# Regrouping a decode-attention kernel: K and V in four 4 MB units, four heads to a score bank, the FFN moved before the last values

## The chip, the cores and the metric

One NeuronCore of one Trainium2 chip; the other cores are idle. The metric is device time in microseconds (us) of one execution. A profile's span is not the time measured for the same execution, so spans are compared with spans here, and times with times.

Engines: PE multiplies matrices, DVE is the vector engine, ACT the scalar engine, POOL sets constants, SP asks for the loads. DMA is 16 engines that all loads share.

An execution is called *slow* when it is over 1.5% longer than the fastest of its kernel.

## The reference, cut to what matters

```python
xn = layernorm(x)                                   # x: (2, 1, 448)
q  = (xn @ wq)                                      # 16 heads of 256
k, v = k_cache[:, :, -2048:], v_cache[:, :, -2048:] # 2 batches, 8 kv heads, 2048 x 256 each
s  = softmax(q . k / 16) . v                        # two q heads share a kv head
s  = s.reshape(2, 1, 4096) @ wo                     # wo: (4096, 448)
g  = silu(relu(xn @ w1) @ w2)                       # w1: (448, 1792)
out = x + s * g
```

All inputs are bf16. K and V are 16.8 MB each, wq and wo 3.7 MB each, w1 and w2 1.6 MB each: 44.1 MB in all, each byte used once. The line of `g` is called the FFN below. The work is small, the bytes are not.

## The kernel before

Every operation is put into a list for its engine, with the operations that it waits for; an engine executes its list in order. A head pair `k` is one kv head for both batches; its K and V come as 1 MB transfers, 8 KB to a partition:

```python
def kv_src(c, cache):
    hkv, b = divmod(c, 2)
    return cache[b, hkv, SK - W:SK, :].rearrange("(p t) d -> p (t d)", t=NT)   # NT = 16
```

K is transposed on PE (`do_T`, four fp32-viewed 128x128 transposes into a bank, a piece of the memory that PE writes to, then one eviction, a copy out of it, by DVE or ACT in turn), multiplied with q (`do_S`, into bank `sbk`), put through a softmax (maximum over all keys by a transpose of the row maxima on PE, bias, exp, sum), and p is transposed and multiplied with V (`do_PV`). Here is the table of steps, which threads the parts of one pair between the transposes of the next ones:

```python
for i in range(NCH * NPAIR):
    at_step(i, 0, lambda i=i: do_T(i))
...
for k in range(NPAIR):
    e = NCH * k                                  # NCH = 8 transpose groups a pair
    at_step(e + 8, 2, lambda k=k: do_S(k, 0))
    at_step(e + 11, 2, lambda k=k: do_S(k, 1))
    at_step(e + 11, 4, lambda k=k: ch_max(k))
    at_step(e + 12, 4, lambda k=k: ch_rmT(k))
    at_step(e + 13, 4, lambda k=k: ch_bias(k))
    at_step(e + 13, 4, lambda k=k: ch_exp(k))
    at_step(e + 16, 4, lambda k=k: ch_Pt(k))
    at_step(e + 17, 4, lambda k=k: ch_sum(k))
    # ... do_PV from step e + 18 on, two of its groups at a time
```

After the last pair come `do_H(0)`, `do_H(1)`, `do_hT`, `do_F` (the FFN: 14 matmuls of 448 columns, seven small ones, 56 of 112), then wo (128 matmuls). The loads are asked for in the order K, V, ..., w1, w2, wo.

Of the kernel before, what the change touches and what calls it, by code (L numbers as in the profile page):

```python
# [5 lines left out]
BF = mybir.dt.bfloat16  # L6
# [70 lines left out]
def bass_recurrent_scan__sliding_block_cached__dense_activation_relu__decode_kernel(  # L77
# [21 lines left out]
    NT = W // 128  # L99
    NPAIR = HKV  # L100
    NCH = 8
    SLOTS = 7
    NKB = 6
    NVB = 8
    NKT = 12
    NP = 3
    HC = HD // 2
    FC = DFF // 2
    WO_PARTS = [10, 10, 8, 2, 2]
    NCOL = D // 4  # L110

    es = contextlib.ExitStack()
    with es:
# [17 lines left out]
        qmask = named("qmask", [128, 4], F32)  # L131
        fold = named("fold", [128, 32], BF)
        gsum = named("gsum", [128, 128], F32)
# [8 lines left out]
        qz = named("qz", [128, 16 * NPAIR], BF)  # L142
# [7 lines left out]
        rm = [named(f"rm{i}", [128, 1], F32) for i in range(2)]  # L150
        mrow = [named(f"mrow{i}", [128, 128], F32) for i in range(2)]
        bias = [named(f"bias{i}", [128, 1], F32) for i in range(2)]
        e_sb = [named(f"e_sb{i}", [128, 512], BF) for i in range(2)]
        ssum = [named(f"ssum{i}", [128, 1], F32) for i in range(2)]
        rs = named("rs", [128, NPAIR], F32)
        pt = [named(f"pt{i}", [128, 64], BF) for i in range(NP)]
        o_sb = [named(f"o_sb{i}", [128, 512], BF) for i in range(2)]
        at_exp = named("at_exp", [128, 256], BF)
        at2 = named("at2", [128, 64], BF)
        wqo = named("wqo", [128, 32 * D], BF)  # L160
        assert SLOTS * HC <= 32 * D
        w1_sb = named("w1_sb", [128, SLOTS * FC], BF)
        w2_sb = named("w2_sb", [128, 14 * D], BF)
        kbuf = [named(f"kbuf{i}", [128, NT * DH], BF) for i in range(NKB)]
        vbuf = [named(f"vbuf{i}", [128, NT * DH], BF) for i in range(NVB)]
        kt = [named(f"kt{i}", [128, 1024], BF) for i in range(NKT)]
# [11 lines left out]
        def kv_src(c, cache):  # L178
            hkv, b = divmod(c, 2)
            return cache[b, hkv, SK - W:SK, :].rearrange("(p t) d -> p (t d)", t=NT)  # L180

# [4 lines left out]
        d_k, d_v = {}, {}  # L186
        last_T, last_PV = {}, {}

        wq_src = A_wq.rearrange("r (hf c) -> (r hf) c", hf=2).rearrange("(p s) c -> p (s c)", s=SLOTS)
        w1_src = B_w1.rearrange("r (hf c) -> (r hf) c", hf=2).rearrange("(p s) c -> p (s c)", s=SLOTS)  # L190
        w2_src = B_w2.rearrange("(hf p j) n -> p hf (j n)", hf=2, j=7)
        wo_src = A_wo.rearrange("(p j) n -> p (j n)", j=32)

        def load_k(c):
            d_k[c] = pr.dma(SP, kbuf[c % NKB][:, :], kv_src(c, A_k_cache), [last_T.get(c - NKB)])

        def load_v(c):
            d_v[c] = pr.dma(SP, vbuf[c % NVB][:, :], kv_src(c, A_v_cache), [last_PV.get(c - NVB)])

        load_k(0)  # L200
        load_k(1)
        d_wq = pr.dma(SP, wqo[:, 0:SLOTS * HC], wq_src)
        load_k(2)
        load_k(3)
# [10 lines left out]
        p_mr = [pr.op(POOL, lambda e, t=t: e.memset(t[0:1, :], 0.0)) for t in mrow][-1]  # L215
        p_qz = pr.op(POOL, lambda e: e.memset(qz[:, :], 0.0), [p_one])

        a_z = [pr.op(ACTE, lambda e, t=t: e.memzero(t[:, :])) for t in (obk[0], sbk, obk[1], fbk)]  # L218
# [20 lines left out]
        def fold_op(e):  # L239
            with nc.allow_low_precision("zeros and ones"):  # L240
                return e.tensor_reduce(out=fold[:, :], in_=view(ident, 0, [[1, 32], [32, 4]]), axis=AX.X, op=ALU.add)
        v_fold = pr.op(DVE, fold_op)
        v_gs = pr.op(DVE, lambda e: e.tensor_copy(
            view(gsum, 0, [[32, 4], [1, 32]]), view(fold, 0, [[0, 4], [1, 32]])), [v_fold])
# [5 lines left out]
        for s in range(SLOTS):  # L250
# [4 lines left out]
            in1=view(par8, 0, [[1, SLOTS], [1, 2], [0, 2]]), op=ALU.mult), [m_xr, v_par8])  # L255

        evac, last_S, freed = {}, {}, set()
        st = {}

        def do_T(i):  # L260
            k, s = divmod(i, NCH)
            c = 2 * k + s // 4
            bank, src = tb[i % 3], kbuf[c % NKB]
            src_f, bank_f = src[:, :].bitcast(F32), bank[:, :].bitcast(F32)
            deps = [d_k[c], p_idf, evac.get(i - 3)]
            for n in range(4):
                lo = (4 * (s % 4) + n) * (DH // 2)
                o = pr.op(PE, lambda e, n=n, lo=lo: e.matmul(  # L268
                    bank_f[:, n * 128:(n + 1) * 128], lhsT=src_f[:, lo:lo + 128], rhs=ident_f[:, :],
                    start=True, stop=True, is_transpose=True), deps)  # L270
                deps = []
            last_T[c] = o
            if s % 4 == 3:
                freed.add((load_k, c))
            dst = kt[i % NKT]
            deps = [o, last_S.get(i - NKT)]
            if i % 2 == 0:
                evac[i] = pr.op(DVE, lambda e: e.tensor_copy(dst[:, :], bank[:, :]), deps)  # L278
            else:
                evac[i] = pr.op(ACTE, lambda e: e.activation(dst[:, :], bank[:, :], ACT.Copy), deps)  # L280

        def do_S(k, b):
            bank = sbk
            deps = [st["q"], a_z[1]] + ([st["exp", k - 1]] if b == 0 and k else [])
            for dhi in range(2):
                lhsT = qz[:, 16 * k + 8 * dhi + 4 * b:16 * k + 8 * dhi + 4 * b + 4]
                for i in range(4):
                    ch = NCH * k + 4 * b + i
                    o = pr.op(PE, mm(bank[32 * i:32 * i + 4, :], lhsT,
                                     view(kt[ch % NKT], dhi, [[2, 512]]),  # L290
                                     b == 0 and dhi == 0, b == 1 and dhi == 1, tile_position=(0, 32 * i)),
                              deps + [evac[ch]])
                    deps = []
            for i in range(4):
                last_S[NCH * k + 4 * b + i] = o
            st["S", k] = o

        def ch_max(k):
            st["rm", k] = pr.op(DVE, lambda e: e.tensor_reduce(  # L299
                out=rm[k % 2][:, :], in_=sbk[:, :], axis=AX.X, op=ALU.max),  # L300
                [st["S", k], st.get(("rmT", k - 2))])

        def ch_rmT(k):
            st["rmT", k] = pr.op(PE, lambda e: e.matmul(
                mbk_ap(0, 128, 1), lhsT=rm[k % 2][:, :], rhs=ident_f[:, :], start=True, stop=True,
                is_transpose=True), [st["rm", k], p_idf, st.get("mbk")])
            st["mrow", k] = st["mbk"] = pr.op(DVE, lambda e: e.tensor_reduce(
                out=view(mrow[k % 2], 0, [[32, 4], [1, 4]], n=1), in_=view(mbk, 0, [[0, 4], [1, 4], [32, 4]], n=1),
                axis=AX.X, op=ALU.max, negate=True), [st["rmT", k], p_mr, st.get(("bias", k - 2))])

        def ch_bias(k):
            st["bias", k] = pr.op(PE, mm(mbk_ap(128, 1), mrow[k % 2][0:1, :], one_f[0:1, :], True, True),
                                  [st["mrow", k], p_one, st["mbk"]])
            st["bsb", k] = st["mbk"] = pr.op(DVE, lambda e: e.tensor_copy(bias[k % 2][:, :], mbk_ap(128, 1)),  # L314
                                 [st["bias", k], st.get(("exp", k - 2))])

        def ch_exp(k):
            st["exp", k] = pr.op(ACTE, lambda e: e.activation(  # L318
                e_sb[k % 2][:, :], sbk[:, :], ACT.Exp, bias=bias[k % 2][:, 0:1],
                accum_out=ssum[k % 2][:, 0:1]), [st["bsb", k], st.get(("Pt", k - 2)), st.get(("gs", k - 2))])  # L320

        def ch_Pt(k):
            deps = [st["exp", k], st["mbk"]]
            for j in range(4):
                o = pr.op(PE, lambda e, j=j: e.matmul(  # L325
                    mb16[:, 512 + 128 * j:640 + 128 * j], lhsT=e_sb[k % 2][:, 128 * j:128 * j + 128],
                    rhs=ident[:, :], start=True, stop=True, is_transpose=True), deps)
                deps = []
            st["Pt", k] = o
            st["pt", k] = st["mbk"] = pr.op(DVE, lambda e: e.tensor_copy(  # L330
                view(pt[k % NP], 0, [[16, 4], [4, 4], [1, 4]]), view(mb16, 512, [[128, 4], [32, 4], [1, 4]])),
                [o, last_PV.get(2 * (k - NP) + 1)])

        def ch_sum(k):
            st["gs", k] = pr.op(PE, mm(mbk_ap(130, 1), gsum[:, :], ssum[k % 2][:, 0:1], True, True),
                                [st["mbk"], v_gs])
            st["rs", k] = st["mbk"] = pr.op(DVE, lambda e: e.reciprocal(rs[:, k:k + 1], mbk_ap(130, 1)), [st["gs", k]])

        def do_PV(k, s):
            b, j = divmod(s, 4)  # L340
            c = 2 * k + b
            bank, src, p = obk[k % 2], vbuf[c % NVB], pt[k % NP]
            deps = [d_v[c], st["pt", k], a_z[2]] + ([st.get(("osb", k - 2)), st["q"]] if s == 0 else [])
            for i in range(4):
                lo = (4 * i + j) * DH
# [195 lines left out]
```

## Time and profile before

| | before |
|---|---|
| time, median of the first 3 runs | 114.7 us (114.49 to 116.66) |
| span of the profiled execution (a slow one) | 115.7 us, mean granted PE clock 0.852 |
| bytes, mean rate | 44.1 MB, 383 GB/s over the span |
| busy: PE, DVE, ACT | 73%, 43%, 38% |

First the page of the kernel before. In part 2 each character is the busy share in tenths of a 2.9 us slice; PEclk is the granted PE clock in tenths of full speed; then DMA's share and its rate in each slice; part 4 is the chain that ended last, as shares of the span.

```profile
span 115.7 us, 2285 instructions
PE   0009946980499799759989966999998695886390
PEclk9999999997559999985999998599999955555559
DMA  2998989999999999999999999999999999999200
GB/s 60 428 486 387 476 374 428 422 425 416 419 428 422 414 431 416 414 422 425 416 408 433 414 419 428 414 419 431 416 411 433 435 409 411 421 422 389 73 6 3
DMA packets 5934, 44.26 MB, mean 383 GB/s; under 512 B 674, under 2 KB 932, under 8 KB 1316
DMA 46%; PE 38%; DVE 6%; ACT 4%; issue 1%; POOL 1%; POOLq 0%
```

DMA is full from the second slice to the 37th, that is to about 107 us, at about 420 GB/s. What is left after that are 8 us. PE has gaps, and its clock falls to 0.5 after one of 5 us (the tenth slice on) and for the whole end.

Next, busy time by stretch of that same execution: start and end in us, length, busy time and number of instructions of PE, weight loads, DVE, ACT and POOL, granted clock, DMA share, GB/s.

```profile
28.00:30.00 2.00, 0.00 (x0) 0.00 (x0) 0.00 (x0) 0.36 (x1) 0.00 (x0) 0.50 1.01 422
32.00:34.00 2.00, 2.00 (x19) 1.58 (x11) 0.46 (x2) 0.08 (x1) 0.00 (x0) 0.50 0.99 410
100.00:102.00 2.00, 1.29 (x5) 0.23 (x4) 0.61 (x1) 0.00 (x0) 0.00 (x0) 0.50 1.03 430
102.00:104.00 2.00, 2.00 (x7) 0.60 (x5) 0.00 (x0) 0.00 (x0) 0.00 (x0) 0.50 0.99 411
```

PE idles at 28 to 30 us and still runs at half clock at 32 to 34, when it is fully busy again. At 100 to 104 us it runs the FFN, at half clock.

### The profile page before, as it was taken

How to read it: one execution, taken by the hardware profiler on the slowest of the kernel's cores; microseconds unless marked ns; L12 is line 12 of the kernel's file. 1: busy time of each engine (PE TensorE's matmuls, PEld its weight loads, DVE VectorE, ACT ScalarE, POOL GpSimd, SP SyncE). 2: the span in 40 equal slices, each digit the busy share in tenths (PEclk: the TensorE clock that was granted, in tenths of full speed). 3: DMA queues.
4: the chain of work that ended last, by engine and by line, in shares of the span. 5: the costliest groups of instructions: out<-in, count | busy, mean ns of one | idle time of the engine just before them, and what ended most of it. 6: DMA issues, size and time to landing. Idle time of an engine off the chain costs nothing.

```text
span 115.7 us, 2285 instructions
## 1 busy us (share of the span) xinstructions
PE 85.0 (73%) x990; PEld 53.7 (46%) x990; DVE 49.4 (43%) x131; ACT 44.4 (38%) x57; POOL 1.9 (2%) x13
## 2 busy tenths in 40 slices
PE   0009946980499799759989966999998695886390
PEld 0009923650275465428556544756665342225280
DVE  2046424560027456523745742565575524113401
ACT  1951650668024834813384380348465010000000
POOL 6000000000000000000000000000000000000000
PEclk9999999997559999985999998599999955555559
DMA  2998989999999999999999999999999999999200
GB/s 60 428 486 387 476 374 428 422 425 416 419 428 422 414 431 416 414 422 425 416 408 433 414 419 428 414 419 431 416 411 433 435 409 411 421 422 389 73 6 3
DMA packets 5934, 44.26 MB, mean 383 GB/s; under 512 B 674, under 2 KB 932, under 8 KB 1316
## 3 DMA queue, kind: packets, MB, share of 16 engines
q1 hardware_dynamic: 5896, 44.11, 91.7%
q8 instruction: 8, 0.13, 0.5%
q14 instruction: 2, 0.02, 0.0%
q10 hardware_dynamic: 28, 0.00, 0.0%
HBM read 44.11 MB, written 0.00 MB: 381 GB/s over the span
## 4 chain that ended last, share of the span: by engine, by line
DMA 46%; PE 38%; DVE 6%; ACT 4%; issue 1%; POOL 1%; POOLq 0%
DMA kbuf<-in_A_k_cache_dram 46%; PE tb L268 13%; PE fbk L247 10%; PE obk L247 6%; PE sbk L247 3%; PE mbk L247 3%; PE mbk L325 2%; ACT L224 1%; ACT L218 1%; DVE xg L227 1%; DVE h_n L404 1%; ACT obk L218 1%; DVE o_sb L355 1%; DVE tmp L427 1%; DVE rm L299 1%
## 5 line engine op out<-in xcount | busy, mean ns | idle before, releaser
L268 PE MATMUL tb<-ident_f,kbuf 128*128 128x128 f32 x256 | 43.7, 307 | 9.8 <-DMA kbuf<-in_A_k_cache_dram 9.8
L280 ACT ACTIVATE kt<-tb 128x1024 bf16<-128x1024 bf16 x32 | 32.6, 1023 | 42.7 <-PE tb L268 42.7
L268 PEld LDWEIGHTS tb<-ident_f,kbuf 128*128 128x128 f32 x256 | 31.8, 158 | 17.5 <-DMA kbuf<-in_A_k_cache_dram 10.9
L278 DVE COPY kt<-tb 128x1024 bf16<-128x1024 bf16 x32 | 22.1, 689 | 23.6 <-PE tb L268 23.6
L247 PE MATMUL obk<-vbuf,pt 128*4 128x256 bf16 x256 | 13.7, 305 | 0.0
L247 PE MATMUL sbk<-kt,qz 128*4 128x512 bf16 x128 | 10.6, 410 | 0.1
L355 DVE TENSOR_SCALAR o_sb<-obk,rs 128x256 bf16<-128x256 f32 x16 | 7.5, 471 | 1.6 <-PE obk L247 1.6
L299 DVE TENSOR_REDUCE rm<-sbk 128x1 f32<-128x512 f32 x8 | 5.5, 692 | 6.0 <-PE sbk L247 6.0
L247 PEld LDWEIGHTS obk<-vbuf,pt 128*4 128x4 bf16 x256 | 4.5, 87 | 5.7 <-issue 3.5
L318 ACT ACTIVATE e_sb<-sbk,bias 128x512 bf16<-128x512 f32 x8 | 5.5, 683 | 3.7 <-DVE bias L314 3.7
L247 PE MATMUL mbk<-ident,xg 2*128 2x2 bf16 x7 | 0.3, 163 | 8.9 <-DVE xg L227 8.9
L247 PE MATMUL fbk<-w_sb,xr 128*4 128x448 bf16 x14 | 5.5, 573 | 0.7 <-DVE h_n L404 0.7
L424 ACT ACTIVATE ea<-fbk 128x112 f32<-128x112 f32 x1 | 0.3, 264 | 14.7 <-PE fbk L247 14.7
L247 PE MATMUL fbk<-wqo,at 128*2 128x112 bf16 x128 | 3.2, 298 | 1.8 <-DVE g_sb L428 1.8
L247 PEld LDWEIGHTS mbk<-ident,xg 2*128 2x128 bf16 x7 | 0.3, 101 | 8.9 <-DVE xg L227 8.9
L330 DVE COPY pt<-mbk 128x64 bf16<-128x64 bf16 x8 | 1.5, 192 | 6.4 <-PE mbk L325 6.4
L325 PE MATMUL mbk<-ident,e_sb 128*128 128x128 bf16 x32 | 4.0, 264 | 0.0
L247 PEld LDWEIGHTS mbk<-ssum,gsum 128*128 128x128 f32 x16 | 3.3, 258 | 1.2 <-DVE pt L330 1.0
L247 PEld LDWEIGHTS fbk<-wqo,at 128*2 128x2 bf16 x128 | 2.9, 124 | 2.1 <-DVE g_sb L428 2.1
L247 PE MATMUL mbk<-ssum,gsum 128*128 128x1 f32 x16 | 3.4, 281 | 0.6 <-DVE pt L330 0.6
L325 PEld LDWEIGHTS mbk<-ident,e_sb 128*128 128x128 bf16 x32 | 2.3, 114 | 2.8 <-DVE kt L278 1.3
L404 DVE TENSOR_SCALAR h_n<-fbk 4x448 bf16<-4x448 f32 x2 | 1.2, 612 | 5.4 <-PE fbk L247 5.4
(65 smaller groups left out, 48.7 us busy)
## 6 DMA issues: line engine op xcount, KB each, us to landing
kbuf<-in_A_k_cache_dram SPq DMA_DIRECT2D x16, 1024.0 KB, 24.5
vbuf<-in_A_v_cache_dram SPq DMA_DIRECT2D x16, 1024.0 KB, 25.5
wqo<-in_A_wq_dram SPq DMA_DIRECT2D x1, 3584.0 KB, 15.0
w_sb<-in_B_w_dram SPq DMA_DIRECT2D x2, 1568.0 KB, 25.9
wqo<-in_A_wo_dram SPq DMA_DIRECT2D x2, 1120.0 KB, 28.4
wqo<-in_A_wo_dram SPq DMA_DIRECT2D x1, 896.0 KB, 27.6
wqo<-in_A_wo_dram SPq DMA_DIRECT2D x2, 224.0 KB, 25.2
x_c<-in_A_x_dram ACTq DMA_DIRECT2D x2, 0.9 KB
```

The source lines that it names most:

```text
L218: a_z = [pr.op(ACTE, lambda e, t=t: e.memzero(t[:, :])) for t in (obk[0], sbk, obk[1], fbk)]
L224: a_sd = pr.op(ACTE, lambda e: e.activation(sd[0:B, 1:2], sd[0:B, 0:1], ACT.Sqrt), [v_ve])
L247: return lambda e: e.matmul(out_ap, lhsT=lhsT, rhs=rhs, start=start, stop=stop, skip_group_check=True, **kw)
L268: o = pr.op(PE, lambda e, n=n, lo=lo: e.matmul(bank_f[:, n * 128:(n + 1) * 128], lhsT=src_f[:, lo:lo + 128], rhs=ident_f[:, :], start=True ...
L278: evac[i] = pr.op(DVE, lambda e: e.tensor_copy(dst[:, :], bank[:, :]), deps)
L280: evac[i] = pr.op(ACTE, lambda e: e.activation(dst[:, :], bank[:, :], ACT.Copy), deps)
L299: st["rm", k] = pr.op(DVE, lambda e: e.tensor_reduce(out=rm[k % 2][:, :], in_=sbk[:, :], axis=AX.X, op=ALU.max), [st["S", k], st.get(("rmT ...
L318: st["exp", k] = pr.op(ACTE, lambda e: e.activation(e_sb[k % 2][:, :], sbk[:, :], ACT.Exp, bias=bias[k % 2][:, 0:1], accum_out=ssum[k % 2] ...
L325: o = pr.op(PE, lambda e, j=j: e.matmul(mb16[:, 512 + 128 * j:640 + 128 * j], lhsT=e_sb[k % 2][:, 128 * j:128 * j + 128], rhs=ident[:, :], ...
L330: st["pt", k] = st["mbk"] = pr.op(DVE, lambda e: e.tensor_copy(view(pt[k % NP], 0, [[16, 4], [4, 4], [1, 4]]), view(mb16, 512, [[128, 4], ...
L355: st["osb", k] = pr.op(DVE, lambda e: e.tensor_scalar(out=o_sb[k % 2][:, cols], in0=obk[k % 2][:, cols], scalar1=rs[:, k:k + 1], scalar2=N ...
L404: st["h_n"] = pr.op(DVE, lambda e: e.tensor_scalar(out=h_n[0:4, u * (FC // 2):(u + 1) * (FC // 2)], in0=fbk[0:4, 0:FC // 2], scalar1=0.0, ...
```

## The change

Its intent: fewer and longer rows (32 KB in place of 8 KB to a partition), four softmaxes in place of eight, values as 128 matmuls of 512 columns in place of 256 of 256, and the FFN before the last values so that only wo follows the last loads. A unit is one batch and four kv heads. Partition `p` holds head `p % 4`, so a column of transposed keys belongs to one of four heads, and rows of scores that belong to another head are masked with -30000 before exp.

The core of the diff (the new constants, masks and index arithmetic are cut):

```diff
-    NPAIR = HKV
-    NCH = 8
+    NU = 4
+    NT = 64
+    NCHUNK = NT // 4
...
-        def kv_src(c, cache):
-            hkv, b = divmod(c, 2)
-            return cache[b, hkv, SK - W:SK, :].rearrange("(p t) d -> p (t d)", t=NT)
+        def kv_src(u, cache):
+            b, v = divmod(u, 2)
+            return cache[b, 4 * v:4 * v + 4, SK - W:SK, :].rearrange("h (r t) d -> r h (t d)", t=NT)
...
-        kbuf = [named(f"kbuf{i}", [128, NT * DH], BF) for i in range(NKB)]    # 6 of 1 MB
-        vbuf = [named(f"vbuf{i}", [128, NT * DH], BF) for i in range(NVB)]    # 8 of 1 MB
+        kbuf = [named(f"kbuf{i}", [128, UW], BF) for i in range(2)]           # 2 of 4 MB
+        vbuf = [named(f"vbuf{i}", [128, UW], BF) for i in range(2)]
+        wq_sb, w1_sb, w2_sb, wo_sb = vbuf[1], kbuf[0], kbuf[0], kbuf[1]       # weights share them
...
-        # the table of steps shown above
+        def scores(u):
+            for i in range(NCHUNK):
+                do_T(u, i)
+                if u and i >= 6 and i % 4 == 2:
+                    do_S(u, (i - 6) // 4)
+            if u == 0:
+                do_q()
+                for g in range(3):
+                    do_S(u, g)
+            do_S(u, 3)
+            softmax(u)            # maximum, masks, row maximum, bias, shift, exp, p transposed, sum
+
+        scores(0)
+        load_k(2)
+        load_v(1)
+        scores(1)
+        load_k(3)
+        values(0)
+        scores(2)
+        # w1, w2 into kbuf[0], after the transposes of unit 2
+        load_v(2)
+        values(1)
+        load_v(3)
+        scores(3)
+        # wo into kbuf[1], after the transposes of unit 3
+        do_H()
+        do_F()
+        values(2)
+        values(3)
+        # then the output projection
```

## The prediction

> **What bounds it now.** The DMA queues. The page's 40 slices show 16 DMA engines at 9 tenths and 405 to 440 GB/s from 3 to about 107 us; 44.1 MB at about 420 GB/s is 105 us. The chain of waits is 46% K loads, 38% PE. The waits view gives 42.7 us of ACT and 23.6 us of DVE idle before key-transpose evictions. After the last bytes only 8 us follow (FFN gate, wo, output). The Trainium skill ("DMA: Bandwidth & Descriptors", "Where 436 GB/s comes from") puts the port ceiling at 435 GB/s, so 32 KB rows can win at most 3 to 4%; the trace's 420 agrees.
>
> **What the change does.** It halves the softmaxes (8 to 4), turns 256 PV matmuls of 256 columns into 128 of 512, and moves FFN work before the last values. But it lays PE's program out serially: each unit's 16 transpose groups, its whole softmax, then values. Before, softmax and PV steps were threaded between the next heads' transposes. And the first transposes wait for 4 MB instead of 1 MB.
>
> **Cost of the PE chain, from durations in the timeline of before.**
> - K0 lands at about 12.3 us by the GB/s by stretch (transposes began at 9.15).
> - Transposes: 0.52 us a group of four at full clock, 0.85 at half. Scores: 0.55 us per eight.
> - Softmax, estimated by adding durations of before: maximum 0.69, two small DVE steps 0.35, transpose and row maximum 0.6, extra copy 0.2, bias 0.55, new 512-column shift 0.7, exp 0.9, transposes of p 0.6, their copy (now 512 columns) 0.65, sum 0.5: about 5.9 us, PE nearly idle. Four times: 24 us, exposed.
> - The Trainium skill ("TensorE: Matmul & The Clock Gate", Part 1) says that an idle window of some 3.4 us halves the clock until a busy window has passed. The trace agrees: idle from 26 to 31 us, granted clock 0.50 until about 34 us. So each softmax costs 1 to 2 us more of cold transposes, and FFN and values after the last softmax run cold.
> - Values: eight groups at 0.43 us cold, scaling 0.7, fold 0.4: 4.7 us.
>
> Sum: first transposes end at 22.6; q and scores 28.3; softmax with table load 35.4; unit 1 scores 48.8, softmax 54.6; values 59.3; unit 2 77.5; values 82.2; unit 3 100.4; FFN 9.1 (as before) 109.5; values of units 2 and 3 119; wo 3.2 and output 4 us: span 126, or 125 as timed (the profile of before was 1 us above its median).
>
> DMA meanwhile: K3 ends at about 71, w1 is released by unit 2's transposes at about 70, wo lands at about 109. The queue hardly starves, but its end no longer sets the time; PE's order does. Row size gains almost nothing.
>
> **Predicted: 124.5 us**, 119 to 129 (8 in 10). Faster by over 2%: 0.03; within 2%: 0.07; slower: 0.90.
>
> **What would show it.** Right: the chain of waits mostly PE, DVE and ACT, K loads only at the start; four PE gaps of 5 to 6 us at the softmaxes, clock 0.5 after them; DMA idle for the last 14 us or so; steady rate 415 to 435 GB/s. Wrong: DMA full to within 8 us of the end; PE waiting for K late; a rate far from 420 (4 MiB between heads in one transfer could slow it).
>
> **What would make it wrong.** PE staying warm through softmaxes and values (4 us less); a shorter softmax chain; a DMA stall where w1 waits for unit 2's transposes, pushing wo past 112 us and making it slower still.

## The result, and the profile after

| | before | after |
|---|---|---|
| median time of 4 runs each | 115.67 us (114.49 to 116.66) | 127.19 us (126.71 to 128.2) |
| span of the profiled execution | 115.7 us (slow) | 124.7 us (fast) |
| mean granted clock there | 0.852 | 0.841 |

The changed kernel is slower: the ratio of the fast runs is 1.108, with a 95% interval of 1.097 to 1.119. Ratios here are the mean time of one kernel's fast runs over that of the other's of the same rounds, so they are not quite the ratios of the medians quoted.

The page of the changed kernel, the same lines as of before:

```profile
span 124.7 us, 1851 instructions
PE   0010799954299993287999626989994277787590
PEclk9999999999959999657999995558999855559965
DMA  5797999979799998989999599998999999400000
GB/s 169 336 505 336 441 441 462 494 342 504 336 504 431 410 494 342 494 370 473 441 399 483 138 404 398 460 496 389 462 426 410 396 414 400 164 8 0 0 5 1
DMA packets 2475, 44.22 MB, mean 355 GB/s; under 512 B 290, under 2 KB 548, under 8 KB 932
PE 55%; DVE 15%; ACT 15%; DMA 10%; issue 3%
```

The chain is now PE, DVE and ACT; DMA's 10% is the wait for the first K. The loads run at full rate to about 107 us, as before, and the last of wo lands at about 110 us (asked for at 95.9 us, 14.1 us to landing); some 15 us follow without any. Between the slices the rates jump (336, 505), and one stretch shown below has a DMA share of 1.22, which is more than can be: probably packets, now larger, are counted in the slice in which they end. The mean is what counts. The single 138 in the 23rd slice (68.6 to 71.7 us) is real: the queue ran nearly empty there, because w1 may be asked for only when the transposes of unit 2 are done (SP asked at 69.6 us).

This is the softmax of unit 1 on the chain that ended last of the changed kernel: start us, duration us, and what; the line numbers are those of the changed kernel.

```profile
47.67 0.64 PE sbk L260 x5
48.34 0.70 DVE rm L306
...
50.36 0.39 PE mbk L260 x2
...
50.97 0.76 DVE s_sb L322
51.75 0.73 ACT e_sb L326 x2
...
52.53 0.62 PE mbk L331 x4
53.17 0.43 DVE pt L336
...
53.65 0.59 PE mbk L260 x2
54.24 3.55 PE obk L260 x24
57.79 0.03 issue
57.81 0.76 DVE o_sb L357
58.58 0.05 issue
58.62 0.26 PE mbk L260 x4
58.88 0.95 PE tb L280 x8
```

The scores end at 48.3 us (47.67 + 0.64), the softmax at 54.24: 5.9 us, in which PE does a transpose, two tiny matmuls, four transposes and two tiny matmuls, and otherwise waits. Then the values (`obk`) take 3.55 us, their scaling 0.76, and only at 58.88 do the next transposes start. And these are the clock and the work there, by stretch, in the changed kernel:

```profile
50.00:52.00 2.00, 0.38 (x2) 0.29 (x2) 1.18 (x4) 0.25 (x1) 0.00 (x0) 0.74 1.22 524
52.00:54.00 2.00, 0.95 (x6) 0.69 (x6) 0.42 (x1) 0.47 (x2) 0.00 (x0) 0.50 1.10 475
54.00:56.00 2.00, 2.00 (x22) 0.87 (x25) 0.17 (x1) 0.00 (x0) 0.00 (x0) 0.50 0.75 315
102.00:104.00 2.00, 2.00 (x7) 0.64 (x5) 0.00 (x0) 0.00 (x0) 0.00 (x0) 0.50 1.02 430
```

PE is busy for 0.38 of 2 us in the softmax; the clock falls to 0.50, and the values at 54 to 56 us run at it. The FFN (102 to 104 us) too.

### The profile page after: what moved, and what is told of

Read it like the earlier page. It is cut to its first block, busy times and chain, and to the rows that moved or that the text cites. A ratio compares the mean times of both kernels' runs of the same rounds, so it can differ in the third digit from the quotient of the medians.

```text
span 124.7 us, 1851 instructions
## 1 busy us (share of the span) xinstructions
PE 80.2 (64%) x810; PEld 50.5 (40%) x810; DVE 47.0 (38%) x107; ACT 40.5 (32%) x48; POOL 2.0 (2%) x11
## 4 chain that ended last, share of the span: by engine, by line
PE 55%; DVE 15%; ACT 15%; DMA 10%; issue 3%
PE tb L280 22%; ACT kt L290 12%; PE obk L260 11%; DMA kbuf<-in_A_k_cache_dram 10%; PE fbk L260 8%; PE sbk L260 7%; PE mbk L260 4%; DVE o_sb L357 2%; DVE s_sb L322 2%; ACT e_sb L326 2%; DVE rm L306 2%; PE mbk L331 2%; DVE pt L336 1%; DVE h_n L403 1%; DVE mrow L314 1%
## 5 line engine op out<-in xcount | busy, mean ns | idle before, releaser
L280 PE MATMUL tb<-ident_f,kbuf 128*128 128x128 f32 x256 | 38.7, 305 | 6.9 <-DMA kbuf<-in_A_k_cache_dram 4.4
L260 PE MATMUL sbk<-kt,qz 128*32 128x512 bf16 x128 | 10.8, 393 | 2.8 <-ACT kt L290 2.3
L260 PE MATMUL obk<-vbuf,pt 128*16 128x512 bf16 x128 | 11.8, 533 | 0.0
L326 ACT ACTIVATE e_sb<-s_sb 128x512 bf16<-128x512 f32 x4 | 2.5, 629 | 18.8 <-DVE s_sb L322 18.8
L331 PE MATMUL mbk<-ident,e_sb 128*128 128x128 bf16 x16 | 2.2, 285 | 7.2 <-ACT e_sb L326 7.2
L357 DVE TENSOR_SCALAR o_sb<-obk,rs 128x512 bf16<-128x512 f32 x4 | 3.0, 750 | 9.1 <-PE obk L260 9.1
L306 DVE TENSOR_REDUCE rm<-sbk 128x4 f32<-128x512 f32 x4 | 2.8, 691 | 8.7 <-PE sbk L260 8.7
L260 PE MATMUL fbk<-kbuf,xr 128*4 128x448 bf16 x14 | 5.5, 572 | 0.7 <-DVE h_n L403 0.7
L260 PEld LDWEIGHTS obk<-vbuf,pt 128*16 128x16 bf16 x128 | 3.7, 114 | 5.4 <-issue 4.4
L260 PEld LDWEIGHTS sbk<-kt,qz 128*32 128x32 bf16 x128 | 2.5, 94 | 6.7 <-ACT kt L290 3.3
```

The source lines that it names most:

```text
L260: return lambda e: e.matmul(out_ap, lhsT=lhsT, rhs=rhs, start=start, stop=stop, skip_group_check=True, **kw)
L280: o = pr.op(PE, lambda e, n=n, lo=lo: e.matmul(bank_f[:, n * 128:(n + 1) * 128], lhsT=src_f[:, lo:lo + 128], rhs=ident_f[:, :], start=True ...
L306: v = pr.op(DVE, lambda e: e.tensor_reduce(out=rm4[:, :], in_=view(sbk, 0, [[1, 4], [4, 128]]), axis=AX.X, op=ALU.max), [st["S", u]])
L326: a = st["exp", u] = pr.op(ACTE, lambda e: e.activation(e_sb[:, :], s_sb[:, :], ACT.Exp, accum_out=ssum[:, 0:1]), [v, st.get(("Pt", u - 1) ...
L331: o = pr.op(PE, lambda e, j=j: e.matmul(mb16[:, 512 + 128 * j:640 + 128 * j], lhsT=e_sb[:, 128 * j:128 * j + 128], rhs=ident[:, :], start= ...
L357: ob = st["osb", u] = pr.op(DVE, lambda e: e.tensor_scalar(out=o_sb[:, :], in0=obk[u % 2][:, :], scalar1=rs[:, u:u + 1], scalar2=None, op0 ...
```

## The experiments

Theory: the serial order of PE's program costs the time, by the softmaxes that PE waits through and by the clock that falls meanwhile; the loads no longer bound the kernel. Rivals: units of 4 MB start late and starve PE or the queue; rows of 32 KB with 4 MiB between heads are slower to load; and, within the theory, that only the waits count and not the clock. Names: the experiments on the changed kernel begin with `a_`, on the kernel before with `b`, loads alone with `d_`. Each call ran on another chip. The changed kernel itself was run in its first call only; the fast runs of the kernel before, 114.16 to 114.72 us over the calls on the other chips, show how little a chip changes (the exceptions stand below the last table).

All experiments passed the check of the result, those of loads alone too, which only write x back. The check says little: in the reference, run on a CPU, the output differs from x by at most 0.0004, where x goes up to 0.14. That the softmaxes compute the right thing is read from the code and not shown by a run.

### The softmax cut short: a_nomax

```diff
-            # rm4, rmm, rm (DVE), transpose (PE), mrow, mall (DVE), bias (PE, DVE)
             v = st["shift", u] = pr.op(DVE, lambda e: e.scalar_tensor_tensor(
-                ... scalar=bias[:, 0:1], in1=view(low, ...), op0=ALU.add, op1=ALU.min),
+                ... scalar=zero_f[:, 0:1], in1=view(low, ...), op0=ALU.add, op1=ALU.add),
```

> The changed kernel without the row maximum (scores here are small, so the result stays right): the 2.6 us from the last scores matmul to the bias copy go from each of the four softmaxes. Serial-PE theory: four times 2.6 us come off the span, about 10 us, to about 117 us as timed, a little more if the clock cools less. Rival, coarse units or long rows hold the loads back: the loads end at about 108 us either way and the time moves by under 2 us.

Measured: 113.66 and 112.95 us in its fast runs, 114.2 median. Against the changed kernel's 127.3 (mean of four) that is 14 us less, for a removed chain of four times 2.6 us. The loads' end moved little: the last wo lands at about 107.5 us, against 110. The serial theory holds, and there is more in it than the waits themselves. Of the 13.1 us between the two profiled spans, the removed waits are 9.5 (in the first softmax only 1.6, because the transposes of unit 1 then wait for K until 32.9 us); the other 3.6 are the balance of faster and slower matmuls at a mean clock of 0.893 in place of 0.841, the FFN alone 1.9 of them (7.4 us in place of 9.3). This version is a probe, not a remedy: without the maximum, larger scores would overflow.

### Loads in pieces of 1 MB: a_rows8k

```diff
         def load_k(u):
-            d_k[u] = pr.dma(SP, kbuf[u % 2][:, :], kv_src(u, A_k_cache), [st.get(("T", u - 2))])
+            for p in range(4):
+                cols = slice(p * UW // 4, (p + 1) * UW // 4)
+                d_k[u, p] = pr.dma(SP, kbuf[u % 2][:, cols], kv_src(u, A_k_cache)[:, :, cols], [st.get(("T", u - 2))])
```

(V likewise; the transposes wait for their piece, values for all four.)

> The changed kernel with each 4 MB load cut into four of 1 MB (8 KB per partition each), each transposed as it lands. Serial-PE theory: the first transposes start at about 9 us in place of 13.2, but q then waits for wq at about 22 us, so only 1.5 to 2 us come off, to about 125 us; the rate stays at about 420 GB/s. Rival, the wait for the first 4 MB is what the change lost: 4 us or more come off. Rival, 32 KB rows with 4 MiB between heads are slow: the rate over the loads rises by several per cent; or they are fast, and it falls.

Measured: 125.91 and 126.69 us in the fast runs, 127.31 median. So of the 1.5 to 2 us that the theory gave it about 1 came, and not the 4 us of the rival; nor did the rate rise (422 GB/s from 30 to 40 us, where the changed kernel has 419). The chain of this kernel around q shows why (the profiled execution is one of the two slow ones, 127.93 us):

```profile
3.64 18.27 DMA vbuf<-in_A_wq_dram
...
21.95 2.93 PE obk L264 x28
...
34.51 1.60 PE tb L284 x7
```

q started at 21.95 us in place of 23.5, but its 28 matmuls took 2.93 us in place of 1.64: PE had finished the first unit's transposes early, waited for wq, and cooled. The second unit's transposes start at 34.5 us, as in the changed kernel (34.6). In this execution the earlier start of the first unit had been lost again by the start of the second; where the 1 us of the fast runs came from, no trace shows.

### The same work in another order: a_threaded

The softmax is cut into five steps, and these and the values of two units ago are put between the next unit's transposes; the FFN's matmuls stand between the steps of the last softmax. Loads and operations are the same.

```diff
+        def stream(u):
+            steps = softmax_steps(u - 1) if u else None
+            for i in range(NCHUNK):
+                do_T(u, i)
+                if u:
+                    if i == 1: do_S(u - 1, 3); steps[0]()      # maximum
+                    if i == 3: steps[1]()                      # its transpose, row maximum
+                    if i == 4: steps[2]()                      # bias, shift, exp
+                    if i == 8: steps[3]()                      # p transposed
+                    if i == 9: steps[4]()                      # sum
+                    if i in (7, 11, 15): do_S(u, (i - 7) // 4)
+                if u > 1:
+                    ...   # do_PV of unit u - 2 at i = 2, 5, 6, 10; scaling at 12; fold at 14
```

> The changed kernel with the same loads and the same operations, but PE's and the other engines' order changed: each softmax and each values step is threaded between the transposes of the next unit, and the FFN's matmuls stand in the gaps of the last softmax. Serial-PE theory: the softmaxes are hidden and the loads bound the kernel again: 111 to 114 us, faster than the kernel before. Rival, coarse units: units of 4 MB starve PE or the queue whatever the order, 120 us or more.

Measured: 115.05 to 115.83 us, four fast runs, median 115.52. This is 12 us below the changed kernel, 1 to 2 us above the upper edge expected. In the same call the kernel before had one fast run (114.39) and six slow ones (116.48 to 117.52), too few fast ones for an interval. So order repairs nearly all of the loss. The chain of a_threaded tells where the last microseconds are:

```profile
47.55 24.41 DMA kbuf<-in_A_k_cache_dram
71.97 0.04 issue
72.01 1.97 PE tb L280 x8
```

K of the last unit was asked for at 47.55 us behind V of the second, and landed at 71.97; all of PE's work on it follows.

### PE kept busy while it waits: a_warm

The changed kernel's order is kept, waits and all. Dummy matmuls into the FFN's bank are put in front of PE's waiting operations, in numbers that fit the waits:

```diff
+        def warm(n):
+            for _ in range(n):
+                pr.op(PE, mm(fbk[:, 0:128], ident[:, :], ident[:, :], True, True), [a_z, p_id])
...
+            warm(12)    # before the transpose of the maxima
+            warm(8)     # before the bias
+            warm(24)    # before p is transposed
+            warm(6)     # before the sum
+            warm(10)    # before the fold, units 0 and 1
```

> The changed kernel with dummy 128x128 matmuls into the FFN bank wherever PE waits in a softmax or for the scaling of values, in numbers that fit the waits (60 per unit). The result stays right. If the cooled clock is a real part of the loss, as the prediction said (1 to 2 us per softmax, FFN and values cold), the granted clock stays near 1.0 and 6 to 9 us come off, to about 119 us. If only the waits themselves count, under 2 us.

Measured: 114.08 to 114.62 us, four fast runs; ratio to the fast runs of before 1.000 (0.998 to 1.003). Some 13 us come off without one wait removed: 127.3 against 114.3. The expectation had the direction and half to two thirds of the size. The page's clock line and the shares of the chain that ended last, and then the same softmax on that chain as shown above:

```profile
PEclk9999999999999999999999999999999999999999
PE 48%; DVE 18%; ACT 17%; DMA 11%; issue 3%
```

```profile
46.18 0.64 PE sbk L260 x5
46.84 0.70 DVE rm L310
...
51.95 0.38 PE mbk L260 x2
52.33 1.86 PE obk L260 x32
54.20 0.03 issue
54.22 0.76 DVE o_sb L365
54.98 0.05 issue
55.03 0.26 PE mbk L260 x4
55.28 0.95 PE tb L284 x8
```

The softmax takes 5.5 us (46.8 to 52.33) in place of 5.9, the values 1.86 in place of 3.55. Added up over the two chains: the values of units 0 and 1 save 1.7 us each, the transposes and scores of units 1 and 3 save 1.2 and 1.5 (those of unit 2 nothing, as the values before them had warmed the clock), three softmaxes 0.4 each, the FFN 3.2 (9.3 to 6.1), the last two values 0.8, wo 1.1: 12.4 us, against a difference of the spans of 12.6.

The waits of 22 us (four of 5.5) are not hidden here: the chain is still PE, DVE and ACT, and its 11% of DMA is again the first K. At full clock this serial chain comes out as long (112.1 us of span) as the kernel before does in its fast state, which is bound by its loads (112.5 us, shown below). The two have different limits, so that they agree so well is chance. The loss needs both: the serial order, and the clock that falls in it. Taking away either one gives nearly all of it back, so the 12 us of one and the 13 of the other can't be added.

### K of the last unit earlier: a_best

```diff
         stream(0)
         load_k(2)
-        load_v(1)
         stream(1)
         load_k(3)
+        load_v(1)
```

(on a_threaded)

> The threaded version with K of the last unit asked for before V of the second one. In the threaded version the last K landed at 72 us and all of PE's work on it, 38 us, followed on the chain. With K 10 us earlier PE has slack, w1 is asked for well before the queue is empty, and only wo is left at the end: about 110 us span, 111 to 112 us as timed, faster than the kernel before in either of its groups. If long rows and large units still cost something, 115 us or more.

Measured: 114.2 to 115.43 us; ratio to before 1.006 (1.000 to 1.012). The expectation was missed by 2 to 3 us. The chain now ends in a load, as meant, but that load is late:

```profile
86.59 22.18 DMA kbuf<-in_A_wo_dram
108.78 0.04 issue
108.82 0.39 PE fbk L260 x8
```

w1 is still asked for only after the transposes of unit 2, at 69.0 us, with the queue's last load landing at 72, and the page's slices there (67 to 73 us) have 360 and 313 GB/s.

### The loads alone: d_units32k, d_heads8k

All computing is cut; each load waits only for the last one into its buffer. For the changed kernel, and in the layout of before:

```diff
-            d_k[u] = pr.dma(SP, kbuf[u % 2][:, :], kv_src(u, A_k_cache), [st.get(("T", u - 2))])
+            d_k[u] = pr.dma(SP, kbuf[u % 2][:, :], kv_src(u, A_k_cache), [d_k.get(u - 2)])
```

> Only the loads of the changed kernel, in its order and layout (32 KB rows, 4 MB units), each buffer refilled as soon as its last load has landed; no compute, so the result is wrong on purpose. The other half of a pair with the same loads in the layout of before. If the row size is worth nothing: 106 to 109 us span for both. If 32 KB rows move more per second, as the rates in the compute runs hint (about 430 against 420 GB/s), this one is 2 to 3 us shorter than the other.

> Only the loads of the kernel before, in its order and layout (8 KB rows, one head of one batch per transfer), no compute, wrong on purpose. Floor of the kernel before: about 108 us span. If 8 KB rows cost rate, it is 2 to 3 us longer than the loads alone of the changed kernel.

> The loads alone of the changed kernel again, beside the loads alone of before on the same chip: same numbers as its first run if the chip plays no part.

Measured: 32 KB rows 110.65 to 110.76 us and, on the chip of the other, 110.71 to 110.74; 8 KB rows 112.02 to 112.14. The changed loads are worth 1.4 us, or 1.2%, and not the 2 to 3 us expected; the last byte lands at 106.1 and 107.8 us. Length of rows, size of transfers and order differ together here, so the part of the rows alone is not shown. The rival that long rows are slow has fallen. Both are floors: the kernel before in its fast state gets its last wo at 107.8 us, the floor of its loads.

### One part of the change alone: b_ffnmid

The kernel before, with w1 and w2 loaded before the last two V pairs and the FFN computed there:

```diff
-        order += ["k6", "k7", "v5", "v6", "v7"]
+        order += ["k6", "k7", "v5", "w1", "w2", "v6", "v7"]
...
+        at_step(65, 6, ffn)      # do_H(0), do_H(1), do_hT, do_F
```

> The kernel before, with one part of the change alone: w1 and w2 are loaded before the last two value pairs, the FFN is computed at that point, and only wo is left at the end of the queue. If the 8 us after the last byte are what the FFN part was aimed at, about 4 us of them go: 110 to 112 us. If FFN placement is worth nothing: 114 to 116 us.

Measured: 114.07, 114.3, 114.57 and 114.88 us. The same call has before at 114.39 once and at 116.48 to 117.52 six times. So the expected 110 to 112 did not come: against the fast group this is nothing, but none of its four runs is in the slow group, and the median falls from 116.73 to 114.43. Four runs are too few to say that the slow group is gone. The chain of b_ffnmid ends in wo's landing at 107.86 us, the floor of these loads, and 4.4 us follow it, against 4.7 in the fast state of the kernel before.

### The kernel before: before_again

> The kernel before, unchanged, to get a trace of one of its fast executions: its times fall in two groups (about 114.4 and 116.7 us) and the profile at hand is of the slower one. If the two groups differ by PE's clock in the part after the last loads, the fast trace shows the same rate of the loads and FFN matmuls that run at more than half clock there, some 2 to 3 us shorter.

Measured: 114.3 and 114.42 (fast), 116.01 and 117.14 (slow); the profile is of a fast execution. Its stretches, to be held against those of the slow one shown before:

```profile
100.00:102.00 2.00, 1.48 (x7) 0.50 (x7) 0.49 (x1) 0.00 (x0) 0.00 (x0) 1.00 1.00 417
102.00:104.00 2.00, 1.53 (x65) 1.32 (x65) 0.64 (x4) 0.00 (x0) 0.00 (x0) 1.00 0.99 414
```

The rate is the same; the FFN's second half runs at 1.00 where the slow execution had 0.50, is done before the last load, and wo's matmuls then follow the landing at 107.8 us, 112.5 us span. In the slow one the FFN's gate came at 109.5 us, after the last load. Why the clock comes back in one execution and not in another of the same program, no run here shows. The traces give a lead. In both executions the granted clock changes only at multiples of some 3.41 us from one another (the slow one falls at 92.18 us and rises at 112.66, six such steps; the fast one falls at 92.85 and rises at 99.67, two). In the fast one PE was busy for 2.92 of the 3.41 us before the rise (85%); in the slow one, in the three steps from 95.59 to 105.83 us, for 2.23, 2.70 and 2.66 (65 to 79%). So it may hang on how the FFN's two bursts and the gap between them fall on these steps. But one step of the slow one, 92.18 to 95.59 us, had 3.13 us busy and no rise after it, so this is not a rule.

### Versions meant to beat both: a_best2, a_best3

a_best2 gives w1 and w2 buffers of their own, asks for them after the first V, does the FFN while PE waits for the third K, and moves the values of the second unit to the end of the last stream.

```diff
+        w1_sb = named("w1_sb", [128, SLOTS * FC], BF)
+        w2_sb = named("w2_sb", [128, 14 * D], BF)
...
-                    if i in (2, 5, 6, 10):
+                    at = (2, 5, 6, 10, 12, 14) if u == 2 else (8, 10, 12, 13, 14, 15)
+                    if i in at[:4]:
```

> The threaded version with buffers of their own for w1 and w2, so that they are asked for right after the first V and wait for nothing, the FFN done while PE waits for the third K, and K of the last unit before V of the second. No load waits for PE with the queue nearly empty, and only values of the last unit and wo follow the last loads. The loads alone took 108.8 us span (110.7 as timed): 109 to 110 us span, 111 to 112 as timed, 2% or more below the fast group of the kernel before (114.3). If the large units still cost something that the order cannot repair, 114 us or more.

Measured: 118.41 us median; ratio to before 1.037 (1.031 to 1.043). A miss. The last V may be asked for only when the values of the second unit are done with its buffer, and I had put those last: SP asked at about 91 us, with the queue empty. In this rate line the 31st and 32nd slices (87 to 93 us) have 23 and 180:

```profile
GB/s 181 361 361 530 327 473 473 361 530 366 439 462 361 425 421 410 514 402 417 462 383 496 406 400 473 383 473 423 372 383 23 180 383 518 355 396 436 384 63 1
```

a_best3 goes back to a_best's order, keeps the buffers of w1 and w2 but asks for them after the second V, and keeps PE busy at its long waits:

```diff
+        warm(60, fbk, [a_z, p_id])      # before stream(1), for the second K
+        warm(80, fbk, [a_z, p_id])      # before stream(2), for the third K
...
+            if u > 1:
+                warm(12, tb[0][:, :].bitcast(F32), [evac[63]])   # before the last two folds
```

> The order of the run a_best (last K before the second V), with the two things that run and the one after it showed: w1 and w2 have buffers of their own and are asked for behind the second V, so no load waits for PE with the queue nearly empty, and the second values step comes early, so the last V is not held back. PE's clock is kept up by dummy matmuls while it waits for the second and third K and for the last two scalings. Loads alone: 108.8 us span. Expected 109 to 110.5 us span, 111 to 112.5 as timed, about 2% under the fast group of the kernel before (114.3). If it stays at 114, the large units cost something else than order and clock.

Measured: 112.96 to 113.91 us, six fast runs, median 113.1, 0.5 to 1.4 us above the range expected; the ratio to the runs of before that are labelled fast is 0.984 (0.978 to 0.990). The profiled execution is the one at 113.91; its span, 111.9 us, is 3 us above the loads alone (108.8). The clock still fell twice, for 6.8 us each time, and the values at 97.87 us ran at half of it. It beats the changed kernel by 14 us. The 1.6% against before flatters it: five of the eight runs of before in that ratio took 115.16 to 115.84 us. Against the other three (114.28 to 114.38) the gain is 1.0 us or 0.9%. It is small, though the slowest run of a_best3 (113.91) is below the fastest of before in any call (114.16); the record's verdict at 2% is "unclear".

| | time (fast runs) | what differs |
|---|---|---|
| changed kernel | 126.71 to 128.2 | |
| a_rows8k | 125.91, 126.69 | loads in 1 MB pieces |
| a_best2 | 118.27 to 119.31 | threaded; last V asked for too late |
| a_threaded | 115.05 to 115.83 | order |
| a_best | 114.2 to 115.43 | order, last K earlier |
| a_warm | 114.08 to 114.62 | clock |
| before | 114.16 to 114.72, slow group about 116.7 | |
| b_ffnmid | 114.07 to 114.88 | FFN before the last V |
| a_nomax | 112.95, 113.66 | shorter softmax |
| a_best3 | 112.96 to 113.91 | order, w1 and w2 early, clock |
| loads alone, 8 KB and 32 KB rows | 112.02 to 112.14, 110.65 to 110.76 | |

(The calls of a_best2 and a_best3 label six runs of before between 115.0 and 115.84 us fast as well; they are left out of the row, but are in the two ratios.)

## Why the prediction was right or wrong, point by point

The prediction, 124.5 us with 119 to 129, held 127.19, and its mechanism is what the runs showed: PE's serial order, with the softmaxes exposed and the clock falling, and the loads ending early. That its sum came within 1.3 us of the span is in part luck: it was 1.5 us short at the end of the FFN and 1.4 us long after the last values. Its sum beside the trace of the changed kernel:

| end of | predicted, us | measured, us |
|---|---|---|
| first K landing | 12.3 | 13.2 |
| transposes of unit 0 | 22.6 | 23.5 |
| q and scores of unit 0 | 28.3 | 28.9 |
| softmax of unit 0 | 35.4 | 34.6 |
| softmax of unit 1 | 54.6 | 54.2 |
| values of unit 0 | 59.3 | 58.9 |
| softmax of unit 2 | 77.5 | 77.25 |
| softmax of unit 3 | 100.4 | 101.8 |
| FFN | 109.5 | 111.0 |
| values of units 2 and 3 | 119 | 117.6 |
| span | 126 | 124.7 |

- *What bounds it now.* Right in kind. But the profile at hand was of a slow execution. "After the last bytes only 8 us follow" is 4.7 us in a fast one (107.8 to 112.5 us).
- *Softmax 5.9 us, four times.* Measured 5.7, 5.9, 5.9, 5.9. The copy of p took 0.43 us, not 0.65; the rest made up for it.
- *"Softmax with table load".* Wrong by 1.3 us. The table was loaded at 24.6 us, while ACT waited for the shift.
- *"1 to 2 us more of cold transposes", FFN and values cold.* The mechanism is right. One term was mis-sized: "PE staying warm through softmaxes and values (4 us less)". a_warm measured 12.6 us of span. I had written down the cold terms one by one (values 4.7 us, FFN 9.1, transposes) and had not added up what they would be warm.
- *Values 9.5 us at the end.* Measured 6.6 (111.0 to 117.6): the clock came back at about 112 us, after the FFN.
- *The profile "1 us above its median", so 125 as timed.* Wrong sign. Time is some 2 us more than the span in every run here; the two numbers compared were of different executions. Without that step the span of 126 gives 128, and the measurement is 127.2.
- *"Row size gains almost nothing".* 1.4 us for the changed loads as a whole, measured by the loads alone: 1.2%, within the 3 to 4% that the prediction estimated as the most, from the page's 435 GB/s and the trace's 420.
- *"The queue hardly starves".* Right: one dip to 138 GB/s where w1 waited, and the last of wo lands at about 110 us, where the prediction had 109.

The Trainium skill's page "TensorE: Matmul & The Clock Gate" (section "Why this matters for your kernels") advises no gaps over about 3 us between bursts of matmuls. Gaps cost the clock: with them filled (a_warm) the granted clock is full throughout, and 12.6 us of span go. But the gaps here were shorter than the page's, and the measurement decides: in the softmax of unit 1 the clock fell at 50.96 us, after gaps of 1.2 and 0.6 us, with PE busy for 1.27 of the last 3.41 us. What the page's Part 1 says of an idle window is thus seen here with a window that is not idle.

## What to carry to other kernels

A latency chain (here maximum, bias, exp, transpose, sum) on an engine that executes in order should be threaded through the next block's independent work (here that took 12 us off the changed kernel); halving the number of chains does not help if they stop being hidden. When such waits remain, count them twice: as waits, and as the half-speed work behind them; filling them with dummy matmuls is a quick test of the second part, and here it gave back 12.6 us. Measure the loads alone first: here that floor (112.1 us for the layout of before) says that the kernel before, at 114.4, had 2% left, and that what an order change must guard is the moment at which each load may be asked for.

## What the Trainium skill lacked or had wrong

- "TensorE: Matmul & The Clock Gate", Part 1, gives some 3.4 us of sustained work as enough for the full clock, and does not say how long the gaps in it may be. In the slow execution of before the FFN's two bursts of 2.8 us, with 0.7 us between them, and the small matmuls after them ran at 0.50 for its whole length of 9 us; in a fast one of the same program the clock was back at 1.00 in 100 to 102 us, after the first burst. What decides between the two, no run here shows (a lead stands under before_again).
- The same page names gaps as a cause of half clock but not dummy work as a cure: 50 or 60 dummy matmuls of 128 columns per unit (220 in all) kept it at full speed and took the span from 124.7 to 112.1 us.
- "DMA: Bandwidth & Descriptors", section "Where 436 GB/s comes from", says that about 358 GB/s per core bind a load from HBM, though its own table has 425 for one transfer of 16 MB. With one core running, 8 KB rows moved about 423 GB/s from 20 to 100 us of the loads alone; "HBM Reference", section "Specifications (TRN2)", has about 425 for a lone core, which agrees.
- "DMA: Bandwidth & Descriptors", table "Measured", goes by the size of a transfer, not by row length. Here 32 KB rows in 4 MB transfers took 110.7 us and 8 KB rows in 1 MB transfers 112.1 us for the same 44.1 MB; these runs don't separate the two either.
- The same page's row "HBM row pitch at large powers of two" (half the rate at a pitch of 4 MiB, for copies between HBM tensors) could be feared for a transfer with 4 MiB between its heads. With 32 rows of 32 KB side by side in each head, the loads alone showed no loss: about 430 GB/s from 20 to 100 us.
